# Attention and routed experts on one core: the first two head pairs loaded and prepared in another way, and the first steps put in another order

## The chip, the cores and the metric

The kernel runs on one core of a Trainium2 chip. The metric is device time in microseconds (us); lower is better. Five engines work side by side, each through its own list of instructions in order: PE (matrix products, with its weight loads PEld), DVE (vector), ACT (scalar functions), POOL (GpSimd) and SP, which here only issues transfers. Transfers issued on SP go through one queue to 16 DMA engines. PE runs at one of two clock levels, 1.2 or 2.4 GHz, shown as a granted clock of 0.50 or 1.00.

## The reference

Attention over 8 batches of 8 heads (576 positions, 64 dimensions), its output read as 4608 tokens of 512 numbers, then a mixture of 8 experts in which each token goes to its best expert alone. In short:

```python
q_rot, k_rot = rotate(q), rotate(k)                 # rotary positions, halves of 32
scores = q_rot @ k_rot.T / sqrt(D)
attn = exp(scores - max); attn /= sum
x = (attn @ v) -> (B*S, H*D)
idx = argmax(x @ w_gate); gate = softmax(x @ w_gate)[idx]
out[idx == e] = gate * (relu(x @ w1[e]) @ w2[e])
```

## The kernel before

The 64 heads are worked as 32 **pairs**, numbered 0 to 31. Every piece of work on a pair is a named **step**; a name is followed here by the pair it works on, as S4 3 for step S4 of pair 3. The last letter of a step in the tables is its engine (p PE, v DVE, a ACT, g POOL, d a transfer on SP); a digit in the names of H and L steps is the head, and L 2 without it means both halves.

For pair n: **FP** loads `qk`, k and q of both heads with the dimensions on partitions (k of the head on partitions 0 to 63, q on 64 to 127), 1.18 MB. **RP** turns them by the rotary angles: six tensor operations, three for each head (lines 375 to 377), into a tile `y`; the product with the sines overwrites the loaded tile. **HK** and **HQ** round `y` to the matrix product's format (the high part), and **L** writes what is left (the low part, line 144). A score is a product over 128 partitions that hold high and low parts, so three transfers bring parts to the other half of the partitions: **DB** copies the high part of k, **DA** the low part of q and **DC** the low part of k; DC writes over what DA reads, so it waits until DA has landed. **cR** collects the last 64 queries of both heads. **S0** to **S8** are the nine score tiles (S4 belongs to both heads, S0 to S3 to the first, S5 to S8 to the second), two score buffers in all; **M** takes the maximum of a tile (DVE, line 432), **E** its exponential and row sums (ACT, line 444). **T** steps transpose on PE, **c** and **K** steps copy, **PN**, **ZR**, **DU** handle the tile of S4; **V**, **U**, **O**, **X** are the product with v and the output; **VP** loads v.

Three things decide the order. PE, DVE, ACT and POOL follow a fixed order: `FIRST`, a list by hand of the first 170 steps, then `setup()` (small copies on DVE, lines 781 to 784, the gate weights `iw` and the index table `xlist` on SP), then `window(w)` for w from 2, which goes through the table `PLAN` (85 steps) with a pair offset for each. The order of transfers on SP is not fixed by these lists: the framework's scheduler puts them where it expects them to be ready, and SP then takes them one after the other, waiting at each for what it needs. Only eight transfers of SP may be under way; the ninth waits for the first.

Buffers tie the steps together. There are two `qk` buffers, so the load of pair n+2 waits for the RP of pair n. There is one `y`, so RP of pair n+1 waits until HK, HQ and L of pair n have read it. From the middle of window 2 on, the order on the engines and on SP is the same in both kernels but for one late index step, and so is the expert part behind it.

At the start the program loads the rotary tables on ACT's queue (`rot`), pair 0, the constants and pair 1 on SP; PE runs 80 small products on ones (`WARM`) meanwhile. DVE does the RP of pair 0, POOL that of all others.

Of the kernel before, what the change touches and what calls it, by code (L numbers as in the profile page):

```python
# [7 lines left out]
F32 = mybir.dt.float32  # L8
# [4 lines left out]
ALU = mybir.AluOpType  # L13
AX = mybir.AxisListType
PSUM = bass.MemoryType.PSUM
P = 128
# [20 lines left out]
]  # L37
FIRST = [
    ("FPd", 0), ("FPd", 1), ("RPv", 0), ("RPg", 1), ("HK0a", 0), ("HQ0a", 0), ("HK1a", 0), ("HQ1a", 0), ("L0v", 0),
    ("L1v", 0), ("DAd", 0), ("DBd", 0), ("DCd", 0), ("VPd", 0), ("cRa", 0), ("HQ1v", 1), ("HK0a", 1), ("HQ0a", 1),  # L40
# [17 lines left out]
]  # L58
GATE = [
    ("gLv", 342), ("gMv", 348), ("gDv", 354), ("gEa", 361), ("gGv", 369), ("gWv", 387), ("gX4a", 390), ("gX0v", 394),  # L60
    ("gX1v", 398), ("gX2v", 401), ("gX3a", 404), ("gSd", 410), ("gQv", 417), ("gBv", 418), ("gOv", 425), ("gPp", 432),
    ("gRv", 436), ("gUv", 445), ("gI0g", 451), ("gI1g", 490), ("gI2g", 527), ("gI3g", 570), ("gI4g", 603),
]
W0 = 2
WARM = 80
CHAINED = ("EngineType.PE", "EngineType.DVE", "EngineType.Activation", "EngineType.Pool")


def const_layout(nb):
    lay, o = {}, 0  # L70
    for name, w in (
        ("ident", 128), ("upper", 128), ("tid", nb * 5), ("valid", 5), ("bad", 5),
        ("escore", 8), ("eid", 8), ("ebase", 8), ("e36", 8), ("tri", 64),
        ("thr1", 8 * 15), ("thr2", 8 * 18), ("slot", NS2 * 8), ("slot2", NS2), ("rot", 2 * 576),
    ):
        lay[name] = (o, w)
        o += w
    return lay, o
# [3 lines left out]
def kernel(  # L82
# [10 lines left out]
    nc = tc.nc  # L93
    B, H, S, D = v.shape
# [5 lines left out]
    lay, CW = const_layout(B)  # L100
# [4 lines left out]
    CR = lay["rot"][0]  # L105
    cst = cpool.tile([P, CR], F32, name="cst")
# [36 lines left out]
    def tt(o, x, y, op):  # L143
        V.tensor_tensor(out=o, in0=x, in1=y, op=op)
# [143 lines left out]
    scattered = []  # L288
# [39 lines left out]
    pp = rctx.enter_context(tc.tile_pool(name="pp", bufs=2, side="right"))  # L328
    ps_t = rctx.enter_context(tc.tile_pool(name="ps_t", bufs=4, space=PSUM, side="right"))
    ld = lctx.enter_context(tc.tile_pool(name="ld", bufs=3))  # L330
    rot = ld.tile([P, 2, S], F32, name="rot", bufs=1)
    nc.scalar.dma_start(out=rot.rearrange("p a s -> p (a s)"), in_=consts[:, CR:CW])
    rp = mctx.enter_context(tc.tile_pool(name="rp", bufs=2, side="right"))
    np_ = mctx.enter_context(tc.tile_pool(name="np", bufs=2, side="right"))
    ps_s = mctx.enter_context(tc.tile_pool(name="ps_s", bufs=2, space=PSUM))
# [31 lines left out]
    npair = B * NP  # L367
    loaded, roped, state, batches = {}, {}, {}, {}

    def do_RP(n, eng):  # L370

        x = loaded.pop(n)
        y = roped[n] = ld.tile([P, 2, S], F32, name="y", bufs=1)
        for h in range(2):
            eng.tensor_tensor(out=y[:, h], in0=x[:, 0, h], in1=rot[:, 0], op=ALU.mult)  # L375
            eng.tensor_tensor(out=x[:, 1, h], in0=x[:, 1, h], in1=rot[:, 1], op=ALU.mult)
            eng.tensor_tensor(out=y[:, h], in0=y[:, h], in1=x[:, 1, h], op=ALU.add)

    def copy(eng, o, i):
        (nc.scalar.copy if eng == "a" else nc.vector.tensor_copy)(out=o, in_=i)  # L380
# [4 lines left out]
    def do_H(st, n, nm, h, eng):  # L385

        if "kT" not in st:
            st["kT"] = [rp.tile([P, 2, S], F32R, name=f"kT{a}") for a in range(2)]
            st["qT"] = rp.tile([P, 2, S], F32R, name="qT")
            st["zt"] = zq[n % 2]  # L390
        copy(eng, (st["kT"][0] if nm == "k" else st["qT"])[:, h], roped[n][:, h])

    def do_L(st, n, h):

        hi, lo = (t[:, h] for t in st["kT"])
        tt(lo, roped[n][:, h], hi.bitcast(F32), ALU.subtract)

    def do_D(st, n, which):

        k0, k1, q0 = (t.bitcast(F32) for t in st["kT"] + [st["qT"]])  # L400
        if which == "A":
            nc.sync.dma_start(out=q0[0:64], in_=k1[64:128])
        else:
            t = k0 if which == "B" else k1
            nc.sync.dma_start(out=t[64:128], in_=t[0:64])
# [164 lines left out]
    def perform(tok, st, n):  # L570

        name, eng = tok[:-1], tok[-1]
        c, a = name[0], name[1:]
        if c == "H":
            do_H(st, n, a[0].lower(), int(a[1]), eng)
        elif c == "L":
            do_L(st, n, int(a))
        elif name == "FP":
            fetch(n)
        elif name == "VP":  # L580
            load_v(n)
        elif name == "RP":
            do_RP(n, nc.gpsimd if eng == "g" else nc.vector)
        elif name in ("DA", "DB", "DC"):
            do_D(st, n, a)
        elif name == "cR":
            do_cR(st, n)
        elif c == "S":
            do_S(st, n, int(a))
        elif c == "M":  # L590
            do_M(st, n, int(a))
        elif c == "E":
            do_E(st, n, int(a))
        elif c == "K":
            do_K(st, n, "AB".index(a), eng)
        elif c == "T" and a[0] in "AB":
            do_T(st, n, "AB".index(a[0]), int(a[1]))
        elif c == "c" and a[0] in "AB":
            do_t(st, n, "AB".index(a[0]), int(a[1]), eng)
        elif c == "V":  # L600
            do_V(st, n, int(a[0]), int(a[1]))
        elif c == "U":
            do_U(st, n, int(a))
        elif c == "O":
            do_O(st, n, int(a))
        elif name in ("X0", "X1"):
            do_X(st, n, int(a))
        elif name in ("c1", "c2"):
            (do_t1, do_t2)[int(a) - 1](st, n, eng)
        else:  # L610
            dict(ZR=do_ZR, PN=do_PN, DU=do_DU, T1=do_T1, T2=do_T2, T3=do_T3, c3=do_t3, RZ=do_RZ, XA=do_XA)[name](st, n)
# [96 lines left out]
                    **{f"gI{c}": listed(c) for c in range(5)}, **{f"gX{c}": scaled(c) for c in range(5)})  # L708

    def first_slots():  # L710
        for s in range(S1):
            indices(s, 2, gi[s % NG])

# [25 lines left out]
    def step(tok, n, ordered):  # L739

        if not 0 <= n < npair or (tok[:-1], n) in done:
            return False
        done.add((tok[:-1], n))
        st = state.setdefault(n, {})
        chained_emit(lambda: perform(tok, st, n), ordered)
        return True
# [19 lines left out]
                    routing.clear()  # L766
                    first_slots()

    step("FPd", 0, False)
    for c0, c1_ in ((0, P), (P, CR)):  # L770
        nc.sync.dma_start(out=cst[:, c0:c1_], in_=consts[:, c0:c1_])
    step("FPd", 1, False)
    iw = cpool.tile([P, NP, 144], F32, name="iw")
    nc.gpsimd.memset(iw, 0.0)
    warm = bank()
    for _ in range(WARM):
        nc.tensor.matmul(warm[:, 0:P], lhsT=onesb, rhs=onesb, start=True, stop=True)
# [31 lines left out]
    DC = DM // P  # L809
# [185 lines left out]
    for w in range(npair, npair + 5):  # L995
        for tok, off in PLAN:
            n = w - off
# [139 lines left out]
```

## Time and profile before

| | |
|---|---|
| time, median of 3 runs (lowest to highest) | 1092.33 us (1090.98 to 1092.63) |
| the profiled execution, its own time | 1082.7 us |
| its span, first to last instruction | 1080.9 us |
| PE busy | 1030.2 us, 95% of the span |
| DVE, ACT, POOL busy | 779.3, 736.0, 440.6 us |

The profiled execution is 9.6 us below the median of the runs, of which 1.8 us lie outside its span. A chain of work is read by following, from a late step, what released each step before it. An idle stretch of PE near the start counts in full if all PE work behind it is closely packed.

### The profile page before, as it was taken

How to read it: one execution, taken by the hardware profiler on the slowest of the kernel's cores; microseconds unless marked ns; L12 is line 12 of the kernel's file. 1: busy time of each engine (PE TensorE's matmuls, PEld its weight loads, DVE VectorE, ACT ScalarE, POOL GpSimd, SP SyncE). 2: the span in 40 equal slices, each digit the busy share in tenths (PEclk: the TensorE clock that was granted, in tenths of full speed). 3: DMA queues.
4: the chain of work that ended last, by engine and by line, in shares of the span. 5: the costliest groups of instructions: out<-in, count | busy, mean ns of one | idle time of the engine just before them, and what ended most of it. 6: DMA issues, size and time to landing. Idle time of an engine off the chain costs nothing. (4 is left out here: it accounts for less than half of the span.)

```text
span 1080.9 us, 21024 instructions
## 1 busy us (share of the span) xinstructions
PE 1030.2 (95%) x7448; PEld 895.7 (83%) x7448; DVE 779.3 (72%) x1448; ACT 736.0 (68%) x1515; POOL 440.6 (41%) x333
## 2 busy tenths in 40 slices
PE   3769999999999999999989999999999999999997
PEld 3658888888888878888777899999999999998886
DVE  3657788797887978879855676666656666655997
ACT  2848898888988889888876445545444555445886
POOL 4535537447374573745442443223333220122110
PEclk7989999999999999999989999999999999999999
DMA  7646446666476676655434215671252520134992
GB/s 257 156 117 169 128 141 168 165 195 130 135 170 164 194 97 169 163 161 160 77 110 146 38 55 176 221 230 56 75 185 69 165 80 20 40 101 146 366 350 88
DMA packets 81858, 157.58 MB, mean 146 GB/s; under 512 B 19607, under 2 KB 52631, under 8 KB 76624
## 3 DMA queue, kind: packets, MB, share of 16 engines
q1 hardware_dynamic: 73600, 135.91, 44.5%
q0 software_dynamic: 8000, 19.65, 5.7%
q8 instruction: 62, 1.02, 0.4%
q14 instruction: 52, 0.43, 0.2%
q10 hardware_dynamic: 144, 0.59, 0.2%
HBM read 160.44 MB, written 20.09 MB: 167 GB/s over the span
## 5 line engine op out<-in xcount | busy, mean ns | idle before, releaser
L432 DVE TENSOR_REDUCE negm<-sp 128x1 f32<-128x576 f32 x288 | 213.6, 751 | 77.6 <-PE sp L427 74.2
L444 ACT ACTIVATE pn<-sp,negm 128x576 f32<-128x576 f32 x256 | 190.8, 745 | 30.7 <-DVE negm L432 27.8
L427 PE MATMUL sp<-kT,qT 128*128 128x288 f32 x1024 | 196.5, 320 | 11.9 <-ACT pn L444 6.4
L427 PEld LDWEIGHTS sp<-kT,qT 128*128 128x128 f32 x1024 | 148.8, 193 | 24.2 <-ACT pn L444 12.0
L375 POOL TENSOR_TENSOR y<-qk,rot 128x576 f32<-128x576 f32 x62 | 88.8, 1432 | 191.3 <-ACT premn L458 107.5
L914 PE MATMUL hp<-xh,w1h 128*128 128x256 f32 x544 | 154.2, 284 | 0.0
L914 PE MATMUL hp<-xl,w1h 128*128 128x256 f32 x544 | 154.0, 283 | 0.0
L914 PE MATMUL hp<-xh,w1l 128*128 128x256 f32 x544 | 153.9, 283 | 0.0
L468 PE MATMUL tp<-cst,pn 128*128 128x128 f32 x1024 | 135.3, 275 | 4.1 <-DVE lgt L558 1.9
L380 ACT COPY PT<-tp 128x512 f32<-128x512 f32 x224 | 130.5, 584 | 10.6 <-PE tp L515 5.4
L515 PE MATMUL tp<-PT,vn 128*64 128x288 f32 x1024 | 137.0, 409 | 0.0
L856 DVE TENSOR_TENSOR w2l<-r,w2h 128x1024 fp32r<-128x1024 f32 x90 | 108.5, 1223 | 35.6 <-ACT w2h L855 34.1
L946 PE MATMUL yp<-w2h,hh 128*128 128x512 f32 x320 | 126.8, 396 | 0.0
L946 PE MATMUL yp<-w2h,hl 128*128 128x512 f32 x320 | 124.9, 390 | 0.0
L946 PE MATMUL yp<-w2l,hh 128*128 128x512 f32 x320 | 124.7, 390 | 0.0
L468 PEld LDWEIGHTS tp<-cst,pn 128*128 128x128 f32 x1024 | 119.2, 141 | 6.3 <-PE tp L468 3.1
L856 DVE TENSOR_TENSOR w1l<-r,w1h 128x1024 fp32r<-128x1024 f32 x92 | 109.9, 1235 | 4.1 <-ACT w1h L855 4.1
L515 PEld LDWEIGHTS tp<-PT,vn 128*64 128x64 f32 x1024 | 70.4, 137 | 49.4 <-ACT pk L380 4.6
L914 PEld LDWEIGHTS hp<-xh,w1h 128*128 128x128 f32 x544 | 104.3, 192 | 1.5 <-issue 0.9
L955 POOL DMA_INDIRECT out_dram<-y,gi x34 | 46.2, 1359 | 145.2 <-DVE y L953 122.1
L914 PEld LDWEIGHTS hp<-xh,w1l 128*128 128x128 f32 x544 | 104.3, 192 | 0.6
L914 PEld LDWEIGHTS hp<-xl,w1h 128*128 128x128 f32 x544 | 104.3, 192 | 0.0
(198 smaller groups left out, 1965.3 us busy)
## 6 DMA issues: line engine op xcount, KB each, us to landing
r<-in_moe_w_dram SPq DMA_DIRECT2D x192, 512.0 KB
qk<-in_qk_dram SPq DMA_DIRECT2D x32, 1152.0 KB
kT<-kT SPq DMA_DIRECT2D x64, 288.0 KB
qT<-kT SPq DMA_DIRECT2D x32, 288.0 KB
vn<-in_v_dram SPq DMA_DIRECT2D x32, 256.0 KB
x_dram<-xt SPq DMA_DIRECT2D x8, 1024.0 KB
vr<-in_v_dram SPq DMA_DIRECT2D x64, 16.0 KB
x_dram<-xr SPq DMA_DIRECT2D x8, 128.0 KB
```

What stands on the lines that cost most here:

```text
L375: eng.tensor_tensor(out=y[:, h], in0=x[:, 0, h], in1=rot[:, 0], op=ALU.mult)
L380: (nc.scalar.copy if eng == "a" else nc.vector.tensor_copy)(out=o, in_=i)
L427: nc.tensor.matmul(sp[:, half, 0:288], lhsT=l, rhs=t[:, h, half * 288:half * 288 + 288], start=(i == 0), stop=(i == len(todo) - 1))
L432: nc.vector.tensor_reduce(out=st["negm"][:, j:j + 1], in_=st["S", j][:, :, 0:288], axis=AX.XY, op=ALU.max, negate=True)
L444: nc.scalar.activation(out=pt.rearrange("p (a b) -> p a b", a=2), in_=st.pop(("S", j))[:, :, 0:288], func=AF.Exp, bias=st["negm"][:, j:j + ...
L468: nc.tensor.transpose(tp[:, i * P:(i + 1) * P], st["pn", h][:, i, kt * P:(kt + 1) * P], ident)
L515: nc.tensor.matmul(st["av", half][r, 0:288], lhsT=st["vn"][:, h, kt, :] if kt < 4 else vr[n % NVR][:, r], rhs=st["PT"][:, h, kt, hs] if kt ...
L856: nc.vector.tensor_tensor(out=lo, in0=src, in1=hi.bitcast(F32), op=ALU.subtract)
L914: m = nc.tensor.matmul(hp[:, fi], lhsT=w[:, dc, fs], rhs=x[:, dc], start=(i == 0), stop=(i == len(prods) - 1))
L946: m = nc.tensor.matmul(yp[t], lhsT=h[:, fi, ts_], rhs=w[:, fi], start=(g == 0 and fi == 0 and i == 0), stop=(g == FQ - 1 and fi == 1 and i ...
L955: sc = nc.gpsimd.indirect_dma_start(out=out, out_offset=bass.IndirectOffsetOnAxis(ap=si[:, t:t + 1], axis=0), in_=y, in_offset=None, bound ...
```

## The change

- The rotary tables, pair 0 and the constants are loaded by eight transfers on SP (`first_loads`): cosines, first head, sines, first head's swapped half, the two pieces of the second head, and the constants in two parts. ACT's queue loads nothing.
- The RP of pair 0 becomes the steps R3 (three operations, first head) and R0, R1, R2 (second head), on DVE as before. Its result goes to a place in a `PT` buffer and not to `y`.
- For pair 0, HK and HQ round 64 partitions each, and DVE writes the low parts straight to where the products read them: LK (k, partitions 0 to 63), LD (k again, partitions 64 to 127), LQ (q, to partitions 0 to 63). DA and DC of pair 0 are gone; DB stays, one transfer for each head (DB0, DB1).
- For pair 1, DA, DB and DC are each split by head (DA0, DA1 and so on).
- `FIRST` is written anew (165 steps). V00 to V04, U0 and RZ of pair 0, TB1 of pair 1, PN and ZR of pair 2, the loads of v for pairs 2 and 3, the RP of pair 4 and the load of pair 5 are no longer in it; the windows do them.
- `WARM` is 130. One step of a late table (`gI4`, 603 to 594) moves.

```diff
-WARM = 80
+WARM = 130
...
-    nc.scalar.dma_start(out=rot.rearrange("p a s -> p (a s)"), in_=consts[:, CR:CW])
...
+    def first_loads():
+
+        x = loaded[0] = ld.tile([P, 2, 2, S], F32, name="qk", bufs=2)
+        for h in range(2):
+            for a in range(2):
+                if h == 0:
+                    nc.sync.dma_start(out=rot[:, a], in_=consts[:, CR + a * S:CR + a * S + S])
+                nc.sync.dma_start(out=x[:, a, h], in_=qk[0, :, a, h])
+        nc.sync.dma_start(out=cst[:, 0:P], in_=consts[:, 0:P])
+        roped[0] = pp.tile([P, 2, 4, 576], F32, name="PT")[:, 0, 0:2]
+
+    def do_R(h, ops):
+
+        x, y = loaded[0], roped[0]
+        if 0 in ops:
+            tt(y[:, h], x[:, 0, h], rot[:, 0], ALU.mult)
+        if 1 in ops:
+            tt(x[:, 1, h], x[:, 1, h], rot[:, 1], ALU.mult)
+        if 2 in ops:
+            tt(y[:, h], y[:, h], x[:, 1, h], ALU.add)
...
-        copy(eng, (st["kT"][0] if nm == "k" else st["qT"])[:, h], roped[n][:, h])
+        r = slice(0, P) if n else slice(0, 64) if nm == "k" else slice(64, P)
+        copy(eng, (st["kT"][0] if nm == "k" else st["qT"])[r, h], roped[n][r, h])
...
-        tt(lo, roped[n][:, h], hi.bitcast(F32), ALU.subtract)
+        q = st["qT"][:, h]
+        a, b = slice(0, 64), slice(64, P)
+        o, i, p = dict(K=(lo[a], hi[a], a), D=(lo[b], hi[a], a), Q=(q[a], q[b], b)).get(part, (lo, hi, slice(0, P)))
+        tt(o, roped[n][p, h], i.bitcast(F32), ALU.subtract)
...
+        if which[1:]:
+            h = int(which[1])
+            k0, k1, q0, which = k0[:, h], k1[:, h], q0[:, h], which[0]
...
-    step("FPd", 0, False)
-    for c0, c1_ in ((0, P), (P, CR)):
-        nc.sync.dma_start(out=cst[:, c0:c1_], in_=consts[:, c0:c1_])
-    step("FPd", 1, False)
+    first_loads()
```

On SP, the stretch before the scores of pair 1, before the change (`qk_253` is FP 2, `qk_323` FP 3, `kT0_228` and `kT1_229` belong to pair 0, `kT0_245`, `kT1_246` and `qT_247` to pair 1):

```order
L357 DMA qk_253<-in_qk_dram 128x2304
L402 DMA qT_230<-kT1_229 64x1152
L405 DMA kT0_228<-kT0_228 64x1152
L405 DMA kT1_229<-kT1_229 64x1152
L357 DMA qk_323<-in_qk_dram 128x2304
L405 DMA kT0_245<-kT0_245 64x1152
L402 DMA qT_247<-kT1_246 64x1152
...
L405 DMA kT1_246<-kT1_246 64x1152
```

And with it (`qk_278`, `qk_327`, `qk_456` and `qk_497` are FP 1 to FP 4, `kT0_271` is pair 0, `kT0_334`, `kT1_335` and `qT_336` are pair 1):

```order
L356 DMA qk_278<-in_qk_dram 128x2304
L434 DMA kT0_271<-kT0_271 64x576
...
L356 DMA qk_456<-in_qk_dram 128x2304
L434 DMA kT0_334<-kT0_334 64x576
L431 DMA qT_336<-kT1_335 64x576
L434 DMA kT0_334<-kT0_334 64x576
L431 DMA qT_336<-kT1_335 64x576
L434 DMA kT1_335<-kT1_335 64x576
L819 DMA iw_133<-in_moe_w_gate_dram 64x4x8
L356 DMA qk_497<-in_qk_dram 128x2304
L434 DMA kT1_335<-kT1_335 64x576
```

DB0 of pair 0 now stands behind FP 1, all copies of pair 1 behind FP 3 (in both kernels FP 3 waits for the RP of pair 1), and the second DC of pair 1 behind FP 4, which waits for the RP of pair 2. Further on, DC 2 stands right behind FP 5 and DC 3 right behind FP 6 in both kernels.

On DVE, from the first operation on the second head of pair 0, with the change (in the kernel before, six operations of RP 0 and the two L of pair 0 stand there, and nothing else before the L of pair 1):

```order
L144 TENSOR_TENSOR PT_132<-qk_124,rot_98 128x576
L144 TENSOR_TENSOR kT1_272<-PT_132,kT0_271 64x576
L144 TENSOR_TENSOR qT_273<-PT_132,qT_273 64x576
L144 TENSOR_TENSOR kT1_272<-PT_132,kT0_271 64x576
L144 TENSOR_TENSOR qk_124<-qk_124,rot_98 128x576
L144 TENSOR_TENSOR PT_132<-PT_132,qk_124 128x576
L461 TENSOR_REDUCE negm_283<-sp_286 128x1
L461 TENSOR_REDUCE negm_283<-sp_292 128x1
L144 TENSOR_TENSOR qT_273<-PT_132,qT_273 64x576
L461 TENSOR_REDUCE negm_283<-sp_311 128x1
L144 TENSOR_TENSOR kT1_272<-PT_132,kT0_271 64x576 x2
```

These are, from the top, R0, LK0, LQ0, LD0, R1, R2, two M, LQ1, M, LD1 and LK1: three more tensor operations than before lie behind the first maxima.

On DVE, around the last L of `FIRST`, before (`kT1_563` is L 3, `sp_570`, `sp_589`, `sp_603` are S4, S2, S0 of pair 2):

```order
L144 TENSOR_TENSOR kT1_563<-y_462,kT0_562 128x576
L432 TENSOR_REDUCE negm_567<-sp_570 128x1
L144 TENSOR_TENSOR kT1_563<-y_462,kT0_562 128x576
L380 COPY pk_509<-pn_529 128x4x64
L432 TENSOR_REDUCE negm_567<-sp_589 128x1
L432 TENSOR_REDUCE negm_567<-sp_603 128x1
```

And with the change (`kT1_621` is L 3, `sp_614`, `sp_631`, `sp_646` are S2, S4, S0 of pair 2):

```order
L461 TENSOR_REDUCE negm_611<-sp_614 128x1
L144 TENSOR_TENSOR kT1_621<-y_524,kT0_620 128x576
L461 TENSOR_REDUCE negm_611<-sp_631 128x1
L402 CAST qT_622<-y_524 128x576
L461 TENSOR_REDUCE negm_611<-sp_646 128x1
L144 TENSOR_TENSOR kT1_621<-y_524,kT0_620 128x576
L814 CAST upb_61<-cst_60 128x128
```

The last L 3 stands behind three maxima of pair 2, not one, and the copies of `setup()` follow it at once.

## Rows read from the trace of the kernel before

**Rows 1.** The page's second part: the span in 40 slices of 27 us, PE's busy tenths and its granted clock in tenths.
```profile
PE   3769999999999999999989999999999999999997
PEclk7989999999999999999989999999999999999999
```
**Rows 2.** Busy time by stretch: the stretch and its length, busy us of PE, PEld, DVE, ACT and POOL (instructions), granted clock, DMA share, GB/s.
```profile
50.00:55.00 5.00, 1.62 (x11) 0.67 (x9) 2.09 (x4) 3.27 (x7) 0.62 (x1) 1.00 0.67 184
55.00:60.00 5.00, 0.87 (x3) 0.88 (x4) 0.00 (x0) 0.00 (x0) 0.00 (x0) 0.55 0.57 142
80.00:85.00 5.00, 4.38 (x31) 3.90 (x32) 3.91 (x8) 4.19 (x13) 4.61 (x4) 1.00 0.69 179
85.00:90.00 5.00, 5.00 (x43) 4.89 (x42) 3.50 (x6) 4.82 (x12) 3.82 (x3) 1.00 0.12 14
```
**Rows 3.** Who PE waited for in the first 90 us: us in total, times, longest.
```profile
PE sp L427 <- DMA kT<-kT: 22.4, 3, 13.6
```
**Rows 4.** The timeline from 40 to 82 us (start, length, instruction): L 2, the first operation of RP 3, FP 5, DC 2 and the table `xlist` on SP, S4 2, the second half of L 3, the first operation of RP 4, FP 6 and DC 3 on SP, S4 3.
```profile
40.37 1.42 DVE L144 TENSOR_TENSOR kT<-y,kT 128x576 fp32r<-128x576 f32 x2
41.87 1.41 POOL L375 TENSOR_TENSOR y<-qk,rot 128x576 f32<-128x576 f32 x1 [8.90 <-DVE kT L144]
50.65 0.35 SPq L357 DMA_DIRECT2D qk<-in_qk_dram  x1
51.09 0.46 SPq L405 DMA_DIRECT2D kT<-kT  x1
51.61 0.58 SPq L788 DMA_DIRECT2D xlist<-mark  x1
59.13 2.05 PE L427 MATMUL sp<-kT,zq 128*128 128x288 f32 x7 [7.51 <-DMA kT<-kT]
61.89 0.75 DVE L144 TENSOR_TENSOR kT<-y,kT 128x576 fp32r<-128x576 f32 x1
62.72 1.42 POOL L375 TENSOR_TENSOR y<-qk,rot 128x576 f32<-128x576 f32 x1 [12.09 <-DVE kT L144]
71.40 0.34 SPq L357 DMA_DIRECT2D qk<-in_qk_dram  x1
71.83 0.46 SPq L405 DMA_DIRECT2D kT<-kT  x1
80.19 1.32 PE L427 MATMUL sp<-kT,zq 128*128 128x288 f32 x8 [0.46 <-ACT pn L444]
```
**Rows 5.** The timeline of the first 25 us: the first operation of RP 0, the first HK, the two ends of RP 1 on POOL, DB 0 and DC 0 on SP, cR 0, the scores that needed DC 0.
```profile
8.08 0.76 DVE L375 TENSOR_TENSOR y<-qk,rot 128x576 f32<-128x576 f32 x1 [6.08 <-DMA qk<-in_qk_dram]
10.33 0.67 ACT L380 CAST kT<-y 128x576 fp32r<-128x576 f32 x1 [7.86 <-DVE y L377]
14.06 1.39 POOL L375 TENSOR_TENSOR y<-qk,rot 128x576 f32<-128x576 f32 x1 [12.28 <-DVE kT L144]
14.54 5.46 SPq L405 DMA_DIRECT2D kT<-kT  x2
19.61 0.30 ACT L409 CAST zq<-qT 128x128 fp32r<-128x128 f32 x1 [5.91 <-DMA qT<-kT]
21.07 1.40 POOL L377 TENSOR_TENSOR y<-y,qk 128x576 f32<-128x576 f32 x1
22.71 2.02 PE L427 MATMUL sp<-kT,zq 128*128 128x288 f32 x7 [1.27 <-DMA kT<-kT]
```
**Rows 6.** What the DMA engines moved: packets and bytes of the first 13 us, then half microseconds in the columns of Rows 2 (the last number is GB/s).
```profile
DMA packets 1152, 3.67 MB, mean 283 GB/s; under 512 B 256, under 2 KB 640, under 8 KB 896
7.50:8.00 0.50, 0.00 (x0) 0.00 (x0) 0.00 (x0) 0.00 (x0) 0.00 (x0) 1.00 1.19 479
11.50:12.00 0.50, 0.00 (x0) 0.00 (x0) 0.47 (x2) 0.08 (x1) 0.00 (x0) 0.50 0.35 85
20.50:21.00 0.50, 0.14 (x1) 0.17 (x1) 0.00 (x0) 0.50 (x1) 0.49 (x1) 0.50 0.75 166
22.00:22.50 0.50, 0.00 (x0) 0.00 (x0) 0.00 (x0) 0.00 (x0) 0.47 (x1) 0.50 0.02 0
77.00:77.50 0.50, 0.50 (x6) 0.32 (x6) 0.50 (x2) 0.46 (x2) 0.00 (x0) 1.00 0.11 19
```
**Rows 7.** The timeline near 167 us: one operation of an RP on POOL, and two operations of one size on DVE, the first beside it.
```profile
167.52 1.42 POOL L376 TENSOR_TENSOR qk<-qk,rot 128x576 f32<-128x576 f32 x1
167.64 1.35 DVE L144 TENSOR_TENSOR eq<-eq,cst 128x40 f32<-128x40 f32 x1
170.38 0.19 DVE L144 TENSOR_TENSOR eq<-eq,bs 128x40 f32<-128x40 f32 x1
```
**Rows 8.** Durations, in the timeline: a copy of `setup()`, a score tile, two T steps (eight products), an E, the reading of its sums, an M.
```profile
68.49 1.62 DVE L784 COPY iw<-cst 128x512 f32<-128x512 f32 x1
65.10 0.79 PE L427 MATMUL sp<-kT,qT 128*128 128x288 f32 x4
64.07 1.04 PE L468 MATMUL tp<-cst,pn 128*128 128x128 f32 x8
72.14 0.75 ACT L444 ACTIVATE pn<-sp,negm 128x576 f32<-128x576 f32 x1
72.77 0.21 ACT L444 ACTIVATION_READ_ACCUMULATOR pn<-sp,negm 128x1 f32 x1
72.67 0.76 DVE L432 TENSOR_REDUCE negm<-sp 128x1 f32<-128x576 f32 x1 [0.50 <-PE sp L427]
```

More of the change, by code (lines that the diff above doesn't have):

```diff
@@ L38 @@
 FIRST = [
-    ("FPd", 0), ("FPd", 1), ("RPv", 0), ("RPg", 1), ("HK0a", 0), ("HQ0a", 0), ("HK1a", 0), ("HQ1a", 0), ("L0v", 0),
-    ("L1v", 0), ("DAd", 0), ("DBd", 0), ("DCd", 0), ("VPd", 0), ("cRa", 0), ("HQ1v", 1), ("HK0a", 1), ("HQ0a", 1),
[17 rows of a table removed]
[18 rows of a table added]
+    ("E0a", 2), ("DBd", 3), ("DAd", 3),
 ]
@@ L61 @@
     ("gX1v", 398), ("gX2v", 401), ("gX3a", 404), ("gSd", 410), ("gQv", 417), ("gBv", 418), ("gOv", 425), ("gPp", 432),
-    ("gRv", 436), ("gUv", 445), ("gI0g", 451), ("gI1g", 490), ("gI2g", 527), ("gI3g", 570), ("gI4g", 603),
+    ("gRv", 436), ("gUv", 445), ("gI0g", 451), ("gI1g", 490), ("gI2g", 527), ("gI3g", 570), ("gI4g", 594),
 ]
 W0 = 2
-WARM = 80
+WARM = 130
 CHAINED = ("EngineType.PE", "EngineType.DVE", "EngineType.Activation", "EngineType.Pool")
@@ L368 @@
     loaded, roped, state, batches = {}, {}, {}, {}
+    def first_loads():
[15 more added lines that the diff above has]
+            tt(y[:, h], y[:, h], x[:, 1, h], ALU.add)
+        if h and 2 in ops:
+            loaded.pop(0)
     def do_RP(n, eng):
@@ L390, in do_H, with do_L @@
             st["zt"] = zq[n % 2]
-        copy(eng, (st["kT"][0] if nm == "k" else st["qT"])[:, h], roped[n][:, h])
-    def do_L(st, n, h):
+        r = slice(0, P) if n else slice(0, 64) if nm == "k" else slice(64, P)
+        copy(eng, (st["kT"][0] if nm == "k" else st["qT"])[r, h], roped[n][r, h])
+    def do_L(st, n, h, part=""):
         hi, lo = (t[:, h] for t in st["kT"])
-        tt(lo, roped[n][:, h], hi.bitcast(F32), ALU.subtract)
+        q = st["qT"][:, h]
+        a, b = slice(0, 64), slice(64, P)
+        o, i, p = dict(K=(lo[a], hi[a], a), D=(lo[b], hi[a], a), Q=(q[a], q[b], b)).get(part, (lo, hi, slice(0, P)))
+        tt(o, roped[n][p, h], i.bitcast(F32), ALU.subtract)
     def do_D(st, n, which):
         k0, k1, q0 = (t.bitcast(F32) for t in st["kT"] + [st["qT"]])
+        if which[1:]:
+            h = int(which[1])
+            k0, k1, q0, which = k0[:, h], k1[:, h], q0[:, h], which[0]
         if which == "A":
@@ L576, in perform @@
         elif c == "L":
-            do_L(st, n, int(a))
+            do_L(st, n, int(a[-1]), a[:-1])
+        elif name in ("R0", "R1", "R2"):
+            do_R(1, [int(a)])
+        elif name == "R3":
+            do_R(0, [0, 1, 2])
+        elif name == "CT":
+            nc.sync.dma_start(out=cst[:, P:CR], in_=consts[:, P:CR])
         elif name == "FP":
@@ L583, in perform @@
             do_RP(n, nc.gpsimd if eng == "g" else nc.vector)
-        elif name in ("DA", "DB", "DC"):
+        elif name[:2] in ("DA", "DB", "DC"):
             do_D(st, n, a)
@@ L710, in first_slots @@
     def first_slots():
+        assert len(scattered) == 5 * (B - 2)
         for s in range(S1):
```

35 rows, old and new, of the table FIRST are left out of this document.

## The prediction

> **What bounds the kernel now.** First the page's slices: PE is full, at full clock, from about 85 us almost to the end; the loss that a change at the start can win back lies in the first slices [rows 1]. Then the stretches: at 80 to 85 us PE works 4.38 of 5 us, from 85 on all of it; before that there are holes, 3.4 us at 50 to 55 and 4.1 at 55 to 60 [rows 2]. So I need one number: when does PE reach the closely packed part. Its first step is S4 3, at 80.19 us before [rows 4], and what PE does from there on is the same list of steps in both kernels. Last, who PE waits for until then: a copy between partition halves, three times, 22.4 us in all [rows 3]. The timeline names the copies [rows 4]: S4 2 starts at 59.13, when DC 2 has landed; DC 2 was issued at 51.09, right behind FP 5 at 50.65; FP 5 waited for the buffer that RP 3 gave back; and RP 3 began at 41.87, when DVE had finished L 2. That is a loop, L to RP to FP to DC to the scores to the next L, and one turn took 20.9 us (L 2 done at 41.79, L 3 at 62.64). Neither kernel's order cuts it, so I follow this loop, not the work of pair 0.
>
> **The early start, and what it is worth.** Pair 0 gets faster. All first loads, 3.67 MB, had moved by some 11.7 us, at up to 479 GB/s [rows 6]; at 430 GB/s on average the flow begins at 3.2. Pair 0 and the tables, 1.77 MB, are then there at 7.3, and RP 0 began at 8.08 [rows 5]: 0.8 us to land. With pieces, the first head needs the first 1.18 MB: there at 5.9, landed at 6.7. The second and third operation of R3 (0.76 us each [rows 5]) end near 8.3, HK0 (0.67 us [rows 5]) near 9.1. DB0 is ready then, but stands behind FP 1 (order on SP): FP 1 ends the first 3.38 MB, at 11.1, and lands near 12, DB0 half a microsecond later. The first scores start near 12.5 instead of 20.86 to 22.71 [rows 5]: 8 to 10 us. The 50 more warming products (some 0.08 us each, 3.8 us) end near 11, inside this wait: they cost nothing, and would cost if DB0 landed before 11. The removed DA, DC and half casts of pair 0 are part of the same 8 to 10 us. But this lead reaches the loop only through pair 1, and there it is spent.
>
> **The loop with the change, step by step.**
> 1. RP 1 on POOL begins when FP 1 has landed, near 12.1 instead of 14.06, since `y` is no longer shared with pair 0. It took 8.4 us (14.06 to 21.07 + 1.40 [rows 5]). Now LQ1, LD1, LK1 and L0 1 run on DVE meanwhile. Beside an operation of POOL, a DVE operation with two inputs in SBUF took 1.35 us and ended as POOL's ended; alone, one of its size takes 0.19 [rows 7]. The two take turns, so each of the four (0.75 us) also holds up POOL's next: 3.0 us, and a fifth, R2, may hit the first. I take 3.5: RP 1 ends at 24.0, later than before. Bounds: 20.6 if none meets, 24.4 with five.
> 2. FP 3 waits for RP 1 and stands ahead of every copy of pair 1 on SP. FP 6 at 71.40 with DC 3 behind it had moved by about 77.2 [rows 4, 6]; with 0.6 us until the wait ends (no data after 22.0, scores at 22.71 [rows 5, 6]) that is 6.4 us: DA0 1 at 30.5. DC0 1 waits for it. DC 0 took 2.7 us from SP's issue at 20.0 to the scores at 22.71 [rows 5]; half the bytes, 2.4: 32.9.
> 3. From there to L 2 done, along the order of ACT, PE and DVE: S1 1 0.8, M 0.75, E 0.93, cR 0.3, E 0.93, HK 0.67, E8 0 0.93, two T 0.9, S3 1 0.8, M 0.75, L 0.75 [rows 5, 8], with 0.35 for the hand-overs: 8.85. L 2 is done at 41.75. Before: 40.37 + 1.42 = 41.79 [rows 4]. The lead is gone.
> 4. RP 3: 8.75 before (from 41.87 until FP 5 went at 50.65 [rows 4]); two more small DVE copies beside it, 0.35: ends at 50.9. FP 5, and DC 2 behind it: before, 8.5 us to the scores, but with `xlist` in the queue [rows 4]; now `xlist` stands far ahead, so the 6.4 of step 2, taken as 6.5: S2 2 starts at 57.4 (before, S4 2 at 59.13).
> 5. PE has been idle some 5 us and starts at 1.2 GHz, as at 59.13, where seven products took 2.05 us [rows 2, 4]. S2, a T step, S4 and S0 come before the third maximum and L 3 (DVE order): 1.05 + 0.9 + 1.85 + 0.8 + 0.75 + 0.75, with 0.4 for hand-overs 6.5 us, against 3.5 before, where L 3 stood behind one maximum. L 3 is done at 63.9; before, 62.64.
> 6. RP 4 takes 9.1 us (8.7 before, 62.72 to FP 6 at 71.40 [rows 4], and PN 2 now beside it), FP 6 and DC 3 the 6.4: S4 3 at 79.5. The other path to S4 3 is ACT's and DVE's work behind `setup()`: its copies meet RP 4 as before (1.62 us for the largest [rows 8]) and end near 67.5 to 68; S4 3 came 10.0 us after their end (68.49 + 1.62 to 80.19), and the steps moved out of `FIRST` (five V, TB1, PN, ZR) add at most 0.5: 78.3. They cost nothing under the wait for DC 3; without it 0.5 us.
>
> So S4 3 moves from 80.19 to 79.5: 0.7 us. ACT and DVE are then some 1 to 2 us ahead of PE, which should take away most of the 0.62 us that PE lost in 80 to 85 [rows 2]. Sum: 1.3 us. Against the profiled execution that is 1082.7 - 1.3 = 1081.4 us; against the median of the runs 1092.33 - 1.3 = **1091.0 us**. The moved index step `gI4` goes into a stretch in which POOL waits: nothing.
>
> **A rule that speaks against the pieces.** At 7.5 to 8 us, with a 64 KB transfer just before in the queue, the engines moved 479 GB/s [rows 6]: transfers under way together hide what each has of fixed time, so I add nothing for eight issues in place of four (some 0.4 us each on SP, which has nothing else to do). The Trainium skill, SBUF — State Buffer, section The DMA setup-cost knee, says that every transfer pays about 2 us whatever its size and advises the largest single transfer. By its figures six pieces one after the other would end near 17 us, an estimate from that page, and the kernel would be some 8 us slower; this trace speaks against adding them up. It would be the second rival, further out.
>
> **The rivals.**
> - *The lead survives.* If DVE's operations fall between POOL's, RP 1 ends at 20.6, all steps move 3.4 us, S4 3 comes at 76.1 to 77 and the kernel takes 1087.6 us. For it: only one row shows the lock so plainly, and the four operations are waited for by others, so their places can shift. Against it: that row, and POOL is busy without a gap from 12 on. Any 1 us won in steps 2 to 5 works the same way.
> - *The pieces load slowly, and the kernel gets slower.* Their runs are 2.3 KB, the whole pair's 9.2. The copies between halves moved 166 GB/s at 20.5 to 21 [rows 6]. At some 200 GB/s the 1.77 MB end at 11.4 instead of 7, FP 1 lands 4.4 us later, and since the loop starts there all of it is kept: -1.3 + 4.4, 1095.4 us. It decides from FP 1 landing at 15.5 on. Against it: of the first 1152 packets 896 were under 8 KB, and those 13 us still moved 283 GB/s, the start included [rows 6].
> - *The change doesn't do what it says*: pair 0 is loaded by pieces, but DB0 or DB1 0 lands behind FP 1 and FP 2 so late that pair 0 is no earlier. Up to 2 us of this stay hidden, because ACT waits for DC0 1 anyway; it would end at 1091 to 1093.
>
> **How the numbers follow.** A measurement of this kernel can tell about 0.2%, 2.2 us. The forecast is a change of less than that: 0.45, and 0.05 for the last rival, whose times lie there too: 0.50. The lead surviving by over 2.2 us needs RP 1 to end before about 23, or as much won elsewhere in the loop: 0.36. Slower by over 2.2 us: 0.08 for slow pieces, 0.06 for a loop step that I have too short (a load with a copy behind it can take 8.5 and not 6.4, as FP 5 did [rows 4]); together 0.14. The range reaches from all of the first rival and a little more, 1087.2, to most of the second, 1094.6.
>
> **What would show it.** Right: first scores at 12 to 13 us; RP 1 from 12 to 23 or 24 with DVE operations of over 1 us beside it; S1 1 at 32 to 33; RP 3 starting within 1 us of 41.8; an idle PE before 57; S4 3 at 79 to 80, ended by DC 3. Wrong: RP 3 starting before 39.5, or FP 1 landing after 14, or S4 3 not waiting for a copy.

## The result, and the profile after

| | before | after |
|---|---|---|
| time, median of 6 runs each (lowest to highest) | 1091.87 us (1090.98 to 1092.63) | 1099.65 us (1094.63 to 1101.50) |
| ratio to the kernel before, 95% interval | | 1.0067 (1.0051 to 1.0084) |
| the profiled execution, span | 1080.9 us | 1095.0 us |

The changed kernel is slower by 0.67%, 7.3 us, where the forecast had a gain of 1.3, and lies above the forecast's range. Its runs also spread over 6.9 us, those of before over 1.7. The kernel before itself took 1090.6 to 1091.9 us in two comparisons (this one and that of e1 to e4) and 1084.4 to 1084.8 in the other three, so kernels of different comparisons are set side by side by their ratios to it.

First the page's slices of the changed kernel, PE's busy tenths and its clock:

```profile
PE   7669999999999999999989999999999999999997
PEclk7889999999999999999999999999999999999999
```

Against [rows 1] the first slice is fuller (7 instead of 3) and the second emptier (6 instead of 7): work came earlier, and part of that was given back. The stretches of [rows 2], in the same columns, show where:

```profile
50.00:55.00 5.00, 2.07 (x13) 1.35 (x10) 3.43 (x8) 4.66 (x12) 0.35 (x1) 1.00 0.68 219
55.00:60.00 5.00, 1.77 (x8) 1.75 (x9) 0.64 (x1) 0.00 (x0) 0.00 (x0) 0.59 0.33 79
80.00:85.00 5.00, 2.87 (x12) 2.86 (x13) 0.76 (x1) 0.00 (x0) 4.79 (x4) 0.50 0.89 170
85.00:90.00 5.00, 4.68 (x33) 4.44 (x32) 3.31 (x6) 4.00 (x10) 0.00 (x0) 0.84 0.77 235
```

From 80 to 90 us PE now works 7.55 us where it worked 9.38, and for half of it at 1.2 GHz (granted clock 0.50), where it had been at 2.4. Who PE waited for in the first 90 us (in all, times, longest; compare [rows 3]):

```profile
PE sp L456 <- DMA kT<-kT: 17.8, 6, 5.1
```

The timeline gives the steps that the forecast walked through: RP 1, the first scores, two operations of DVE beside RP 1, FP 3, S1 1, RP 3, FP 5 and DC 2, S2 2, RP 4, FP 6, then DC 3 and DB 4 in one row, DA 4, the load of v of pair 4, the second product of S4 3, twelve products of T steps behind it:

```profile
14.31 1.40 POOL L397 TENSOR_TENSOR y<-qk,rot 128x576 f32<-128x576 f32 x1 [12.54 <-DMA qk<-in_qk_dram]
14.64 1.99 PE L456 MATMUL sp<-kT,qT 128*128 128x288 f32 x8 [4.42 <-DMA kT<-kT]
20.11 2.83 DVE L144 TENSOR_TENSOR kT<-PT,kT 64x576 fp32r<-64x576 f32 x2 [0.27 <-ACT kT L402]
20.41 1.92 POOL L398 TENSOR_TENSOR qk<-qk,rot 128x576 f32<-128x576 f32 x1
24.25 0.33 SPq L356 DMA_DIRECT2D qk<-in_qk_dram  x1
33.55 0.67 PE L456 MATMUL sp<-kT,qT 128*128 128x288 f32 x3 [0.94 <-DMA kT<-kT]
41.88 1.40 POOL L397 TENSOR_TENSOR y<-qk,rot 128x576 f32<-128x576 f32 x1 [4.28 <-DVE kT L144]
50.38 0.35 SPq L356 DMA_DIRECT2D qk<-in_qk_dram  x1
50.81 0.46 SPq L434 DMA_DIRECT2D kT<-kT  x1
58.23 1.09 PE L456 MATMUL sp<-kT,qT 128*128 128x288 f32 x3 [5.09 <-DMA kT<-kT]
64.67 1.43 POOL L397 TENSOR_TENSOR y<-qk,rot 128x576 f32<-128x576 f32 x1 [14.31 <-DVE kT L144]
73.47 0.35 SPq L356 DMA_DIRECT2D qk<-in_qk_dram  x1
73.91 2.38 SPq L434 DMA_DIRECT2D kT<-kT  x2
76.40 1.00 SPq L431 DMA_DIRECT2D qT<-kT  x1
77.50 1.53 SPq L361 DMA_DIRECT2D vn<-in_v_dram  x1
82.13 2.05 PE L456 MATMUL sp<-kT,zq 128*128 128x288 f32 x7 [4.24 <-DMA kT<-kT]
84.93 2.31 PE L497 MATMUL tp<-cst,pn 128*128 128x128 f32 x12
```

RP 3 starts at 41.88, as before to a hundredth [rows 4]: the lead of 6 us in the first scores was spent on the way, as forecast. What follows was not: S4 3 comes 1.9 us later than before, at the lower clock. In three more traces of the new start with the old order on SP (e2, e5, e14, below) it comes at 80.89 to 82.19. In the kernel before, the twelve products of T steps take 1.47 us, against 2.31:

```profile
81.87 1.47 PE L468 MATMUL tp<-cst,pn 128*128 128x128 f32 x12
```

From the middle of window 2 on PE has the same products in both kernels, so a product can be found in every trace by counting back from the last one. One such product, at 90.06 us in the first trace of before, starts at 89.38 to 90.37 us in seven traces with the old start, and at 92.65 to 94.22 in five with the new one (all with the old order on SP): the start loses some 3.7 us. The rest of the 7.3 us must lie far behind it, where the forecast saw nothing change. Counting back further shows a jump of 2.8 us near 391 us: there PE, DVE and ACT of the changed kernel stand still together. The same products of PE, in the kernel before and (some 7 us later) in the changed one:

```profile
391.11 0.77 PE L427 MATMUL sp<-kT,qT 128*128 128x288 f32 x4
397.92 0.79 PE L456 MATMUL sp<-kT,qT 128*128 128x288 f32 x4 [1.84 <-PE tp L497]
```

### The profile page after: what moved, and what is told of

Its sections match the earlier page's. It is cut to its first block, busy times and chain, and to the rows that moved or that the text cites. A ratio compares the mean times of both kernels' runs of the same rounds, so it can differ in the third digit from the quotient of the medians.

```text
span 1095.0 us, 21142 instructions
## 1 busy us (share of the span) xinstructions
PE 1041.2 (95%) x7498; PEld 905.2 (83%) x7498; DVE 782.6 (71%) x1451; ACT 735.9 (67%) x1516; POOL 440.4 (40%) x333
## 4 chain that ended last, share of the span: by engine, by line
PE 57%; issue 8%; DMA 4%; DVE 2%; ACT 2%; another core or an unknown queue 1%; POOL 1%; SPq 0%; POOLq 0%; ACTq 0%
PE yp L979 15%; PE hp L947 15%; PE sp L456 9%; PE tp L544 8%; PE tp L497 5%; DMA out_dram<-y,gi 3%; PE tp L563 2%; PE xps L902 1%; POOL out_dram L988 1%; DVE negm L461 1%; DMA r<-in_moe_w_dram 1%; PE tp L521 1%; PE tp L511 1%; ACT pn L473 1%
## 5 line engine op out<-in xcount | busy, mean ns | idle before, releaser
L456 PE MATMUL sp<-kT,qT 128*128 128x288 f32 x1024 | 198.9, 322 | 22.6 <-DMA kT<-kT 10.4
L497 PE MATMUL tp<-cst,pn 128*128 128x128 f32 x1024 | 138.0, 278 | 5.1 <-ACT PT L402 3.0
L497 PEld LDWEIGHTS tp<-cst,pn 128*128 128x128 f32 x1024 | 121.9, 144 | 7.4 <-ACT PT L402 3.2
L915 ACT ACTIVATE hh<-hp 128x512 fp32r<-128x512 f32 x68 | 40.6, 597 | 98.4 <-PE hp L947 84.6
```

Source lines behind the costliest of these rows:

```text
L456: nc.tensor.matmul(sp[:, half, 0:288], lhsT=l, rhs=t[:, h, half * 288:half * 288 + 288], start=(i == 0), stop=(i == len(todo) - 1))
L497: nc.tensor.transpose(tp[:, i * P:(i + 1) * P], st["pn", h][:, i, kt * P:(kt + 1) * P], ident)
L915: nc.scalar.activation(out=hh, in_=hp, func=AF.Relu)
```

## The experiments

Theory A: the loss is made in the first 100 us, by copies that wait behind loads. Theory B: by the moved index step. Theories F and G came later, for the stop near 391 us. Ratios are to the kernel before in the same comparison.

**e1, the kernel before unchanged, for a trace at the time of the comparison.** No edit.

> The kernel before, unchanged, to have a trace whose time belongs to the runs that the changed kernel was compared with (the trace shown of before is of an execution of 1082.7 us, its median is 1092). Theory A (the loss is made in the first 100 us): S4 3 starts near 80.2 us again, and from there to the end this execution is within 4 us of the changed kernel's; the 9 us between 1082.7 and 1092 then lie behind 100 us and have nothing to do with the change. Theory B (the loss is made between attention and experts, by the moved index step): this trace keeps PE full between 600 and 660 us, as the first trace does (20.00 of 20 us in each window), and the changed kernel's 4.8 us of holes there are its own.

Ratio 1.0001 (0.9992 to 1.0010), span 1089.6 us. S4 3 starts at 79.50. Counted back, this trace is level with the first one of before to within 0.8 us until 557 us, and loses 8.2 us between 600 and 662 us (of the first trace), in small holes that the changed kernel has too (8.1 us). So those holes, which the first trace lacks, are not the change's: that half of theory B falls. All traces of this comparison have them (6.8 to 8.2 us) and none of the eleven of the other three comparisons, in which the kernel before is 6 to 7 us shorter: they go with the comparison, not with a kernel. They are also most of the 9.6 us by which the first trace's execution lies below its median; the 1.8 us outside the span are no part of these. Against this trace the changed kernel's is 4.2 us late at 90 us and 4.9 at the end.

**e2, the changed kernel with the index step back; e3, the kernel before with the index step alone.**

```diff
-    ... ("gI3g", 570), ("gI4g", 594),      (e2; without the assert)
+    ... ("gI3g", 570), ("gI4g", 603),
-    ... ("gI3g", 570), ("gI4g", 603),      (e3)
+    ... ("gI3g", 570), ("gI4g", 594),
```

> The changed kernel with its last index step back at its old place (603). Theory A (the start): no difference from the changed kernel, 1098 to 1101 us. Theory B (the index step): the holes between 600 and 660 us go, about 4 us less, 1095 to 1096.

> The kernel before with the index step alone moved to 594. Theory A: no difference, 1091 to 1093 us. Theory B: about 4 us more, 1095 to 1096.

e2: 1.0111 (1.0095 to 1.0126). e3: 0.9960 (0.9947 to 0.9974). Both theories were wrong: the moved step gains 0.4%, some 4 us, in either kernel (e2 against the change, e3 against before). The timeline of e1 shows what it had cost, the scatter of 128 index entries on POOL, then ACT's rounding of the first expert weights and the T step that stands behind it:

```profile
549.19 1.03 POOL L697 DMA_INDIRECT xlist<-tid,lpi  x1 [0.30 <-issue]
559.02 1.04 ACT L989 CAST w1h<-r 128x1024 fp32r<-128x1024 f32 x1 [4.06 <-DMA r<-in_moe_w_dram]
560.60 1.12 PE L468 MATMUL tp<-cst,pn 128*128 128x128 f32 x4 [4.62 <-ACT PT L380]
```

The first weight loads go out on SP from 546.68 on, beside this scatter. In e3 the scatter is done some 20 us earlier, before the weight loads are issued, and the same two wait less:

```profile
556.15 1.04 ACT L989 CAST w1h<-r 128x1024 fp32r<-128x1024 f32 x1 [1.11 <-DMA r<-in_moe_w_dram]
557.74 0.66 PE L468 MATMUL tp<-cst,pn 128*128 128x128 f32 x4 [1.25 <-ACT PT L380]
```

Between 535 and 590 us ACT waits 4.7 to 6.9 us in all for these weights in the seven traces with the step at its old place, and 2.1 to 5.0 in the ten with the new one. That the scatter's own transfers hold the weights back is an inference: only its place was changed.

**e4, the changed kernel with FP 5 behind DC 2 and FP 6 behind DC 3 on SP.** `copied` holds the last copy of each pair; the added dependency orders SP's list and waits for nothing.

```diff
-        nc.sync.dma_start(out=loaded[n], in_=qk[n])
+        f = nc.sync.dma_start(out=loaded[n], in_=qk[n])
+        if n in BEHIND:                     # {5: 2, 6: 3}
+            tc.add_manual_dep(f.ins, copied[BEHIND[n]], <NoSync>, ...)
```

> The changed kernel with SP's order altered at two places: FP 5 behind DC 2, FP 6 behind DC 3 (the copies that PE waits for stand ahead of the loads). Theory A (PE waits for a copy that is queued behind a load which waits for POOL): DC 2 goes when L 2 is done, near 45.6 instead of 50.8; S2 2 starts near 51 instead of 58.2, L 3 is done near 57, S4 3 waits for no copy and starts near 75; 7 us less than the changed kernel, 1092 to 1093. Rival (ACT and DVE bound this stretch anyway, the copy only ends last): S4 3 near 80, 2 to 3 us less, 1096 to 1097.

0.9973 (0.9963 to 0.9983): 0.94% below the changed kernel, more than expected. DC 2 goes at 49.02 (not 45.6: it must wait for DA 2 to land), the load after it, and S4 3 waits for no copy:

```profile
49.02 0.46 SPq L439 DMA_DIRECT2D kT<-kT  x1
49.57 0.54 SPq L357 DMA_DIRECT2D qk<-in_qk_dram  x1
70.20 1.33 PE L462 MATMUL sp<-kT,zq 128*128 128x288 f32 x8
```

S4 3 starts at 70.20 instead of 82.13, at full clock, and the common product 13.7 us earlier. Theory A holds for the start.

**e5, 20 one-element writes on DVE and 24 one-element copies on ACT at the start of the changed kernel; e6, the kernel before with the changed kernel's count of instructions on PE, DVE and ACT.**

```diff
+    def pads():
+        pad = cpool.tile([P, 4], F32, name="pad")
+        nc.vector.memset(pad[:, 0:1], 0.0)
+        for _ in range(19):                                            # e6: 3
+            nc.vector.memset(pad[0:1, 1:2], 0.0)
+        for _ in range(24):                                            # e6: 3
+            nc.scalar.copy(out=pad[0:1, 3:4], in_=pad[0:1, 0:1])
-WARM = 80                                                              (e6)
+WARM = 130
```

> The changed kernel with 20 one-element writes on DVE and 24 one-element copies on ACT at the very start, where both engines wait for the first load: nothing is computed differently, but every later instruction of DVE and ACT lies 20 and 24 places further back in the program. Theory F (the stop near 395 us, in which DVE, ACT and PE stand still together, is a wait for instructions, and its place depends on where the code lies): the stop goes or moves, the time falls by 2 to 5 us to 1095 to 1098. Rival G (the stop comes from what the DMA engines do at this place of the program, or from the time at which it is reached): it stays at the same step, and the time stays at 1098 to 1101.

> The kernel before with the changed kernel's count of instructions (4 one-element writes on DVE and 3 one-element copies on ACT at the start, 130 warming products instead of 80), and nothing else of the change. Theory F: the stop near 395 us appears, 2 to 5 us more, 1093 to 1096; the start is as before, S4 3 near 80. Rival G: no stop, 1090 to 1092. If the 50 more warming products cost anything by themselves, S4 3 comes later than 80.2.

e5: 1.0049 (1.0031 to 1.0067); the long wait at that step is gone, and waits of 0.93 and 1.30 us stand before and after it. The interval meets that of the change, so the time decides nothing. e6: 1.0048 (1.0034 to 1.0062); its start is as before (the common product at 89.55), and at the very step PE now waits 3.80 us. The stop comes with the longer program alone, without the new start.

**e7, DB 4 and DA 4 held back until DC 3 has landed.**

```diff
+        if n == 4 and which in "AB":
+            tc.add_manual_dep(f.ins, copied["C", 3], <Sync>, ...)
```

> The changed kernel with the two copies DB 4 and DA 4 held back on SP until DC 3 has landed. Theory C (DC 3 took 8.2 us and not the 6.4 of the forecast because the copies and the V load of pair 4 now go out 2 to 5 us behind it and share the DMA engines): S4 3 starts near 80.4 instead of 82.1, 1.7 us less. Rival (a load with a copy behind it takes 8 us here whatever follows): S4 3 stays near 82.

1.0065 (1.0048 to 1.0081), no gain. DC 3 and then DB 4, which now waits, in one row, and S4 3:

```profile
75.78 7.60 SPq L434 DMA_DIRECT2D kT<-kT  x2
82.89 1.83 PE L461 MATMUL sp<-kT,zq 128*128 128x288 f32 x7 [3.13 <-DMA kT<-kT]
```

S4 3 came at 82.89, near where the rival put it and not at theory C's 80.4. But RP 3 began 1.3 us later in this execution, which hides a gain: DC 3 took 7.1 us from its issue to the scores, against 8.2 with the other transfers behind it. Counted from the load ahead of it, as the forecast did, the pair took 7.6 us (FP 6 went at 75.34), against 8.7 in the changed kernel, 8.2 to 8.6 in e2, e5 and e14, which have its order, and 6.4 in the forecast. So about half of the error goes with the later transfers, as far as one trace of e7 can tell, and the other half is there without them: theory C is right by half at most. The Trainium skill, DMA: Bandwidth & Descriptors, section Issuing engines are not separate DMA queues, says that transfers of different issuing engines run on the same 16 DMA engines and interleave. Here all of them come from SP, so the 8.2 against 7.1 us agrees with the sharing of the engines only.

**e8, the changed kernel with all copies of pairs 1 to 4 ahead of the loads.** As e4, with `BEHIND = {3: 1, 4: 1, 5: 2, 6: 3, 7: 4}`.

> The changed kernel with the copies ahead of the loads from pair 1 on: FP 3 and FP 4 behind the last copy of pair 1, FP 5 behind DC 2, FP 6 behind DC 3, FP 7 behind DC 4. Theory A: the scores of pair 1 start near 30 instead of 33.5 us, all later steps of the loop follow, S4 3 near 72 (75 or 76 with only FP 5 and FP 6 moved): 2 to 3 us less than with those two alone, 1085 to 1086. Rival (ACT and DVE bound the stretch from 33 to 50 us): no less than with those two, 1087 to 1089.

0.9933 (0.9915 to 0.9950). PE's wait for copies in the first 90 us falls from 17.8 to 4.7 us, and most of that is the first scores; S4 3 starts at 68.09 (expected 72), and theory A holds here too, with 0.40% less than e4:

```profile
PE sp L462 <- DMA kT<-kT: 4.7, 3, 3.3
```

**e9, the kernel before with 130 warming products; e10, with four one-element writes on DVE; e13, with 208 warming products.**

```diff
-WARM = 80
+WARM = 130        (e9; e13: 208)
```

> The kernel before with 130 warming products instead of 80, and nothing else. If the stop near 391 us comes from the moved code of DVE and ACT: no stop, ratio 0.999 to 1.001. If it comes from PE's code lying 100 instructions further back: the stop is there, ratio 1.003 to 1.005. If the 50 products cost something at the start: S4 3 later than 80.2 us.

> The kernel before with four one-element writes on DVE at the start, and nothing else. If the stop comes from DVE's code lying four instructions further back: it is there, with DVE's 694th or 695th instruction at its end, ratio 1.003 to 1.005. If it needs ACT's or PE's shift: no stop, ratio 0.999 to 1.001.

> The kernel before with 208 warming products instead of 80: PE's later code lies 256 instructions (each product is a load and a product) further back, which is one whole piece of 16 KB as PE's code is fetched by its queue in the trace. If the stop near 391 us depends on where in a piece PE stands when the DMA engines are slow (in the kernel before a piece was fetched right in that stretch, with 100 instructions more some 6 us ahead of it): the pieces fall as in the kernel before, no stop, ratio 0.999 to 1.001. If any longer code or any later warming brings it: stop, ratio 1.004 to 1.006. The products end near 16 us, before the first scores at 20.8, so they cost nothing themselves.

e9: 1.0061 (1.0043 to 1.0080). e10: 0.9998 (0.9985 to 1.0010). e13: 1.0007 (0.9995 to 1.0018). Fifty products more, which end at 10.8 us, 10 us before PE's next work, cost 6 us in all; 3.4 of them are the wait at 391 us, and 1.3 the products right behind it, which run at 1.2 GHz (granted clock 0.50 from 395.3 to 397.3 us). Products to a count of 208, 128 more, cost nothing. The timeline of e9 at the stop:

```profile
390.04 0.19 ACT L444 ACTIVATION_READ_ACCUMULATOR pn<-sp,negm 128x1 f32 x1
391.09 1.03 PE L468 MATMUL tp<-cst,pn 128*128 128x128 f32 x8
392.04 1.01 POOL L697 DMA_INDIRECT xlist<-tid,lpi  x1 [0.15 <-issue]
393.90 0.59 ACT L380 COPY PT<-tp 128x512 f32<-128x512 f32 x1 [3.67 <-remote]
395.27 1.09 PE L427 MATMUL sp<-kT,qT 128*128 128x288 f32 x3 [3.15 <-ACT pn L444]
395.28 0.76 DVE L432 TENSOR_REDUCE negm<-sp 128x1 f32<-128x576 f32 x1 [4.60 <-remote]
```

ACT stops first, after 390.2, then DVE, and no releaser is found for either ("remote"); PE follows because it waits for ACT; POOL goes on. The trace also holds the transfers that bring code: pieces of 16 KB in one queue, one for each 256 instructions of PE. Around 385 us, at a batch's end, transfers are slow for some 5 us: single packets of the copies between halves, 0.36 us otherwise, take up to 6.1 to 8.6, depending on the trace. Where PE's piece falls against that stretch goes with the stop: there is none when a piece is fetched within it and takes long. This holds in all traces but e15 and the two with the pads of e5 (e5, e12); some of them:

| kernel | warming products | PE's piece fetched at, took (us) | PE's wait at the step (us) |
|---|---|---|---|
| before, first trace | 80 | 384.8, 6.2 | none |
| e13 | 208 | 383.7, 5.6 | none |
| e14 (below) | 80 | 388.9, 7.5 | none |
| e9 | 130 | 378.9, 0.9 | 3.15 |
| e6 | 130 | 377.4, 0.9 | 3.80 |
| after | 130 | 382.6, 0.9 | 1.84 |
| e2 | 130 | 383.0, 0.9 | 5.25 |
| e15 (below) | 80 | 370.1, 7.4 | 3.37, eight products on |

A step of 256 instructions takes the stop away again, as if the place within a piece counted; only the counts 80, 130 and 208 were run, and e15 does not fit. The Trainium skill, Runtime: NRT & Kernel Launch, section Instruction fetch mechanics, says that engines fetch code in blocks of 16 KiB, 256 instructions, through DMA, and that crossing a block is mostly hidden; PE's 16 KB pieces agree with it, while the second queue that brings code has pieces of 8 KB. Whether the 6 us are such a crossing is open: no row names what ACT and DVE wait for. The transfers speak against a wait for code rather than for it: in e9 no piece of either queue lies between 379.8 us, when PE's had come, and 396.9, so none came in while ACT and DVE stood still. In none of the eight traces with the stop does a piece of 8 KB come in while DVE stands still, and only in e2 and e4 one before ACT goes on.

**e14, the changed kernel with 80 warming products.**

> The changed kernel with 80 warming products as before. If the 50 more products cost their 4 to 6 us through the stop here too: no stop, ratio 1.001 to 1.003 (the start's 4 us, less the index step's 3), against 1.0067 for the whole change. Rival (the stop comes with the new start's other instructions too): stop, ratio 1.006 to 1.007.

1.0017 (1.0004 to 1.0030), no stop in its trace. So 0.5% of the change's 0.67%, known to some 0.2, is the 50 products. The trace is of the shortest of its runs, which spread over 5.8 us; whether the longer ones have a stop is not known.

**e11, the kernel before with copies first (as e8; FP 3 also moved behind DC 1 in `FIRST`) and the index step at 594; e12, e8 with the pads of e5; e15, e8 with 80 warming products.**

> The kernel before, old start and all, with the two cheap things alone: the copies of pairs 1 to 4 ahead of the loads on SP, and the index step at 594. If the new start is worth nothing by itself (the loop L, RP, FP, DC sets the end): the wait of 21 us for copies falls to under 13, S4 3 near 70, ratio 0.988 to 0.991, below the 0.9933 of the changed kernel with the same order of copies, which has the stop as well. If the new start is worth its 6 us of earlier scores once the copies no longer wait: S4 3 near 75, ratio 0.993 to 0.996.

> The changed kernel with both mends: copies ahead of the loads (as before, ratio 0.9933 without the other), and 20 and 24 one-element instructions on DVE and ACT at the start, which move the code away from the stop. If the stop costs 2 to 5 us in that kernel too (its trace has 4.1 us at the step): ratio 0.989 to 0.991. If it only moves elsewhere: 0.993.

> The changed kernel with the copies of pairs 1 to 4 ahead of the loads and 80 warming products. Without the stop 4 us less than with 130 (0.9933): ratio 0.988 to 0.990. If the new start is worth its 4 us of earlier scores over the old one (the kernel before with the same two mends: 0.9873, PE's closely packed part 4.3 us later than here): ratio 0.984 to 0.986.

e11: 0.9873 (0.9852 to 0.9895). e12: 0.9876 (0.9855 to 0.9898), 0.57% below e8, with waits of 0.7 to 1.1 us in place of the stop's 3.97. e15: **0.9827 (0.9811 to 0.9843)**, 1066.5 us against 1084.4, the best of all and faster than both kernels. PE's wait for copies in e11, where 12.3 us are the late first scores:

```profile
PE sp L433 <- DMA kT<-kT: 13.7, 2, 12.3
```

The common product starts at 81.7 us in e11 and at 75.5 in e15: once no copy waits behind a load, the new start is worth 6 us there and 0.46%, 5 us, in all, known to some 3. In the profiled execution of e15 PE still has a wait of 3.37 us, eight products further on than the stop, so 80 products do not rule it out with this order. That execution was the longest of the five (1070.9 us, the others 1063.7 to 1067.1); whether the others lack the stop is not known.

## Why the prediction was wrong, point by point

- **What bounds it, and that the lead of pair 0 is spent before RP 3:** right. RP 3 starts at 41.88 (forecast 41.75), S1 1 at 33.55 (32.9), and e4 and e8 show that the loop with a copy behind a load was the bound. That the time of RP 3 came out to 0.1 us is luck in part, as the next point shows.
- **The early start:** the pieces did not add up to the late start that a fixed price for each would give, and the first head was ready as forecast (HK0 done at 9.21; forecast 9.1). But FP 1 landed at 14.3, not 12, which was one of my signs of being wrong, and the first scores came at 14.64, not 12.5. From 3 to 7 us the DMA engines moved some 310 GB/s, and 395 in the kernel before: the rival of slow pieces was right in part. FP 1 is short of the 15.5 from which it decides, and step 1 hid the delay: RP 1 then took 9.9 us instead of 11.9, with three operations lengthened to 1.8 to 1.9 us and two of DVE's small ones beside them in 2.83. Two errors of 2 us cancelled at FP 3 (24.25; forecast 24.1).
- **Step 4, the same term as in step 6:** FP 5 and DC 2 took 7.9 us to the scores, not 6.5, and RP 3 ended 0.5 us sooner: S2 2 at 58.23 instead of 57.4. Step 5 was right (6.4 us from S2 2 to RP 4; forecast 6.5).
- **Step 6 failed.** "FP 6 and DC 3 the 6.4" took 8.7 from FP 6 to S4 3; S4 3 came at 82.13, not 79.5. DC 3 has DB 4, DA 4 and a load of v close behind it, and e7 puts some 1.1 of the 2.3 us down to them; in the kernel before they went out only after 79 us, when the data of DC 3 had been moved (77.2). The other half is the term itself: I took 6.4 from the time at which data stopped flowing and set aside the row that measured a load with a copy behind it, 8.5, because `xlist` stood in the queue there. It is the small rival that I gave 0.06.
- **The clock, a term left out.** I let S4 3 wait for a copy and still took 0.62 us off for 80 to 85 us. PE was idle 4.24 us before it and then ran at 1.2 GHz: from S4 3 to the end of the twelve T products it took 5.1 us, against 3.2 before (from 80.19 [rows 4]; there the twelve start at 81.87 and take 1.47). Together 1.9 us late and some 1.6 to 1.9 for the clock: the start's 3.5 us in the profiled pair, 3.7 over all traces, where I had a gain of 1.3.
- **The moved index step, forecast as "nothing",** was wrong by 4 us in the other direction (e2, e3). I looked at whether POOL waits there, and not at what the DMA engines carry.
- **The 50 more warming products, of which I wrote "they cost nothing",** were wrong by 0.5% (e9, e14). On the path that I looked at, the start, they do cost nothing (e9: the common product at 89.8). The premise that what stands behind window 2 is the same, because its order is the same, is what failed: the same order was not the same time. Why a longer program stops at 391 us stays open.
- **A slip that decided nothing:** in the rival of slow pieces, 1.77 MB at 200 GB/s from 3.2 us on end at 12.0 and not at 11.4, so FP 1 would have come 4.7 us later, not 4.4.

By ratios: +0.50% for the products (e14 against the change), -0.40% for the index step (e3), and what is left of the 0.67%, +0.57%, for the new start. That is 6 us, known to some 2, and more than the 3.7 that the traces show at 90 us; where the rest lies was not found; stops in longer runs of e14 would be counted in it. The spread of the changed kernel's runs fits the stop, whose wait took 1.8 to 5.3 us in the seven traces with 130 products and without the pads of e5; that too is an inference.

## What to carry to other kernels

When PE waits for a short transfer, look at what stands ahead of it in its queue: a load that itself waits for a buffer must not stand before a copy that someone waits for, and setting that order by hand was worth 1.3% here (e8 against the change), the whole rebuilt start 0.5%, and that only once the order was set (e15 against e11). A change that only makes the program longer is not free by that alone: before a small loss is put down to the change's idea, measure the same number of instructions with no work in them. Before a scatter of tiny entries is placed, look at what the DMA engines carry at the time, and not only at whether its own engine is idle: its place was worth 0.4% here (e3).

## What the runs showed of the hardware that was not expected

- Lengthening PE's code by 100 instructions that run in idle time cost 0.61% (e9), by 256 nothing (e13, 1.0007). What ACT and DVE wait for at the stop stays open; more code on these two moved it (e5, and e12 against e8: 0.9876 against 0.9933).
- At each batch's end from 182 us on, every 68 us, the longest packets of the copies between halves took 2.7 to 5.2 us instead of 0.36, and near 385 us 6.1 to 8.6, in every trace.
- With one scatter of 128 entries right behind two gathers on POOL, while the first weight loads go out, ACT's longest wait for the weights was 4.06 us (e1), and with the scatter 20 us earlier the same wait was 1.11 (e3).
